# Value blocks mixed per batch from strided weights, in place of pairs of batches from a channel-major copy

## The chip, the cores and the metric

The kernel runs on one core of a Trainium2 chip. The metric is the device time in microseconds (us); several runs are taken and their median is given.

## What is computed

Four batches, eight heads, 768 tokens of 64 channels. The tokens of a head are cut into 8 blocks of 96. A small 8x8 matrix per head (`sort_net`) is made nearly doubly stochastic by five rounds of exp and of row and column normalisation, and then mixes the blocks of k and v; attention runs inside each block, and a gated feed-forward layer follows.

```python
for _ in range(5):
    P = np.exp(P - P.max(-1)); P = P / P.sum(-1); P = P / P.sum(-2)
k_sorted = np.einsum('bhij,bhjcd->bhicd', P, k_b)
v_sorted = np.einsum('bhij,bhjcd->bhicd', P, v_b)
attn = softmax(scale * q_b @ k_sorted.T)          # within a block of 96
x = (attn @ v_sorted)  as 3072 tokens x 512
out = (silu(x @ w_gate) * (x @ w_val)) @ w_out    # 512 -> 1536 -> 512
```

## The kernel before, in words

Natural tiles hold one row per (head, block), so 64 partitions for a batch, and 96 tokens x 64 channels (`C`, `D`) along each partition. `load_kq` (L78) puts k of a batch in partitions 0 to 63 and q in 64 to 127; `load_v` (L85) puts the two batches of a pair in the two halves. All these loads, which convert float32 to bfloat16, and the weights' (`load_w`, wo) are issued from GpSimd's queue in the order of the text: kq0, v of pair 0, w_gate and w_val in six pieces each, kq1, w_out, kq2, v of pair 1, kq3. `natp` has two buffers, `vnp` one.

The normalisation (L131 to L138) runs on ScalarE and VectorE at the start, and its result is spread by 16 small matmuls (L148) into `rmix` and `vmix`, zero-padded mixing matrices: `rmix[b]` for k and q (L154), `vmix[p]` for a pair's v (L159).

Mixing and transposing are one matmul: a natural slice is the weight, a mixing matrix moves.

- `emit_kq(b)` (L185): for each of the 96 token positions, the 64 channels are the weight columns (next to each other in memory), with two matmuls into the two halves of the partitions. Eight positions fill a PSUM tile `tkq`, and `drain` copies it into `kqt`. There are 12 drains a batch.
- `emit_v(pair)` (L206): for each channel, the tokens are the weight columns. `emit_vch` (L199) first copies the natural tile into `vch`, channel-major, so that they lie next to each other; a row of `vch` is padded from 96 to 128 with zeros (L119). VectorE makes the four copies of pair 0, GpSimd those of pair 1. Then 64 matmuls of 128 rows, 128 weight columns and 128 moving columns (two batches x 8 heads x 8 blocks) fill 16 PSUM tiles `tv` of four channels, each drained into `vt`, which has a 65th column of ones for the softmax sum.

`drain` (L178) takes VectorE and ScalarE in turn. The tiles `tkq`, `tv`, `qk`, `x_ps` and `w_ps` share three PSUM buffers (tag `att`).

`emit_qk` (L221) makes the scores of two heads for four blocks: weights of 64 rows, 128 columns (96 used, the other 32 are the next block's or a pad), and exp on ScalarE into `e_ring`, whose rows have a zeroed pad. `emit_av` (L240) multiplies by `vt`, divides by the sum, and transposes into `xt`. `emit_gv` (L282) is the gate and value layer, `emit_out` (L303) the output layer with its stores.

`emit_att(b)` (L261) emits the keys, then eight units of `emit_qk` and, two units behind, `emit_av`; after the second unit `emit_v` is emitted, in batches 0 and 2 alone. The last loop emits attention of batch b+1 ahead of the feed-forward of batch b. The order on each engine is set by a scheduler at build time, from the dependencies and its own estimates: it puts `g_ps` and `v_ps` matmuls of one batch between the attention steps of the next. On the chip each engine then works in that order.

Of the kernel before, what the change touches and what calls it, by code (L numbers as in the profile page):

```python
# [9 lines left out]
FP32 = mybir.dt.float32  # L10
# [7 lines left out]
def kernel(  # L18
# [36 lines left out]
    natp = ctx.enter_context(tc.tile_pool(name="natp", bufs=2))  # L55
    vnp = ctx.enter_context(tc.tile_pool(name="vnp", bufs=1))
# [28 lines left out]
    def load_v(pair, parts):  # L85
        t = vnp.tile([128, C, D], BF16, name=f"v{pair}", tag="vn")
        step = C // parts
        for s in range(parts):
            for u in range(2):
                nc.gpsimd.dma_start(out=t[u * R:(u + 1) * R, s * step:(s + 1) * step],  # L90
                                    in_=v_nat[2 * pair + u, :, s * step:(s + 1) * step])
        v_tiles[pair] = t
# [24 lines left out]
    vmix = [const.tile([128, 2, H, NB], BF16, name=f"vmix{p}") for p in range(B // 2)]  # L117
    vch = const.tile([128, D, 128], BF16, name="vch")
    nc.vector.memset(vch[:, :, C:], 0.0)  # L119
    for p in range(B // 2):  # L120
        nc.vector.memset(vmix[p], 0.0)
# [5 lines left out]
    load_v(0, 2)  # L127
# [23 lines left out]
    for b in range(B):  # L151
        wk = w_ps[0:R, :, b].unsqueeze(1).to_broadcast([R, H2, NB])
        for two in range(2):
            nc.vector.tensor_tensor(  # L154
                rmix[b][0:R, two, 0],
                mask[0:R].rearrange("p (g two) -> p two g", two=2)[:, two].unsqueeze(2).to_broadcast([R, H2, NB]),
                wk, op=ALU.mult)
        lo = (b % 2) * R
        nc.vector.tensor_tensor(  # L159
            vmix[b // 2][lo:lo + R, b % 2],  # L160
            mask[lo:lo + R].unsqueeze(2).to_broadcast([R, H, NB]),
            w_ps[lo:lo + R, :, b].unsqueeze(1).to_broadcast([R, H, NB]), op=ALU.mult)
# [7 lines left out]
    load_kq(1, [0, 48, 96])  # L170
    nc.gpsimd.dma_start(out=wo_sb, in_=wo_dram)
    load_kq(2, [0, 48, 96])
    load_v(1, 2)
    load_kq(3, [0, 48, 96])

    tog = [0]

    def drain(dst, src):  # L178
        if tog[0] % 2 == 0:
            nc.vector.tensor_copy(dst, src)  # L180
        else:
            nc.scalar.copy(dst, src)  # L182
        tog[0] += 1
# [15 lines left out]
    def emit_vch(pair):  # L199
        nat = v_tiles[pair]  # L200
        for s in range(4):
            cs = slice(s * (C // 4), (s + 1) * (C // 4))
            eng = nc.gpsimd if pair else nc.vector
            eng.tensor_copy(vch[:, :, cs], nat[:, cs, :].transpose([0, 2, 1]))  # L204

    def emit_v(pair):  # L206
        emit_vch(pair)
        dst = vtp.tile([C, 2 * H * NB, D + 1], BF16, name=f"vt{pair}", tag="vt")
        nc.vector.memset(dst[:, :, D:D + 1], 1.0)
        mix = vmix[pair].rearrange("p u a b -> p (u a b)")  # L210
        for db in range(D // 4):
            tp = psum.tile([128, 4, 2 * H * NB], FP32, name="tv", tag="att")
            for ld in range(4):
                nc.tensor.matmul(tp[:, ld, :], lhsT=vch[:, db * 4 + ld, :],  # L214
                                 rhs=mix, start=True, stop=True)
            drain(dst[:, :, ts(db, 4)], tp[0:C].transpose([0, 2, 1]))
        return dst.rearrange("p (u h i) d -> p u h i d", u=2, h=H)

    vts = {}
# [41 lines left out]
    def emit_att(b):  # L261
# [4 lines left out]
        for half, g in units:  # L266
# [3 lines left out]
            if vt is None and len(pend) == 2:  # L270
                if b % 2 == 0:
                    vts[b // 2] = emit_v(b // 2)
                vt = vts[b // 2][:, b % 2]
# [79 lines left out]
```

## Time and profile before

| what | value |
|---|---|
| median of three runs (lowest, highest) | 287.63 us (286.65, 287.9) |
| the profiled execution's own time | 287.63 us |
| its span, first to last instruction | 285.9 us |
| mean granted TensorE clock | 0.968 |
| matmul groups g_ps, v_ps, o_ps (L288, L297, L308) | 84.8, 82.1, 62.4 us busy |
| tkq, qk, av_ps, tv, x_ps (L193, L230, L245, L214, L255) | 20.3, 14.0, 14.9, 12.4, 11.5 us busy |
| drains of tv into vt: VectorE, ScalarE | 16 x 785 ns, 16 x 787 ns |
| drains of tkq into kqt: VectorE, ScalarE | 24 x 688 ns, 24 x 586 ns |
| GpSimd DMA loads | 14.16 MB written, slices 1 to 10 |

A group line names the source line, the engine, the operation, what it writes and reads, shapes, and the number; after the bar its busy time, the mean of one in ns, and the engine's idle time before it. PE is TensorE's matmul, PEld its weight load, DVE VectorE, ACT ScalarE, POOL GpSimd. A matmul's own duration contains the way through the array, and matmuls overlap; the spacing of a run of n is the run's time less one's duration, over n - 1. A timeline line has the start, the time of a run of like instructions, and in brackets the engine's idle time before it with what ended it. Slices are fortieths of the span; a line of a stretch has the stretch, then each engine's busy time and count, the granted clock, the DMA share and GB/s.

### The profile page before, as it was taken

What the parts mean: (1) busy time and instruction counts of PE and PEld (TensorE: products, weight loads), DVE (VectorE), ACT (ScalarE), POOL (GpSimd) and SP (SyncE); (2) the same over time, 40 slices, a digit from 0 to 9 for tenths busy, and PEclk for the clock granted to TensorE, in tenths of its full rate; (3) what the DMA queues carried; (4) which work ended last, traced back from release to release, by engine and by line L of the source; (5) the groups of instructions that cost most, each with busy time, mean ns of one, the idle gap of its engine ahead of it and who ended that gap; (6) DMA issues with size and microseconds to landing.
All of it is one profiled execution on the core that took longest, in us unless ns stands there. A gap on an engine that the chain in (4) does not pass through costs nothing.

```text
span 285.9 us, 6221 instructions
## 1 busy us (share of the span) xinstructions
PE 257.2 (90%) x2600; PEld 152.7 (53%) x2608; DVE 178.9 (63%) x383; ACT 121.7 (43%) x246; POOL 39.1 (14%) x51
## 2 busy tenths in 40 slices
PE   0077799969999999999999999999999999999993
PEld 0066555746655446666655446666555445555441
DVE  6798746937988205789988304699885018888300
ACT  2036745437633215976534215764332134343211
POOL 8557421029500000000000000000000000000000
PEclk9999955979999999999999999999999999999999
DMA  6999999999100122000000122000000220000021
GB/s 99 198 203 197 200 213 204 220 214 214 38 0 1 39 110 76 2 2 0 3 0 2 38 110 76 2 2 2 0 0 2 111 102 10 0 0 3 37 110 73
DMA packets 13659, 20.84 MB, mean 73 GB/s; under 512 B 1088, under 2 KB 8768, under 8 KB 13632
## 3 DMA queue, kind: packets, MB, share of 16 engines
q0 software_dynamic: 10128, 14.16, 28.2%
q1 hardware_dynamic: 3504, 6.30, 5.8%
q8 instruction: 20, 0.33, 0.4%
q14 instruction: 7, 0.06, 0.1%
HBM read 28.32 MB, written 6.29 MB: 121 GB/s over the span
## 4 chain that ended last, share of the span: by engine, by line
PE 82%; DVE 11%; ACT 3%; issue 2%; ACTq 0%
PE v_ps L297 22%; PE g_ps L288 22%; PE o_ps L308 22%; PE av_ps L245 4%; PE qk L230 4%; PE tkq L193 3%; PE x_ps L255 3%; PE tv L214 3%; DVE kqt L180 2%; DVE vch L204 1%; DVE st L251 1%; ACT vt L182 1%; DVE vt L180 1%; ACT th_sb L291 1%; DVE colred L136 0%
## 5 line engine op out<-in xcount | busy, mean ns | idle before, releaser
L288 PE MATMUL g_ps<-xt,wg_sb 128*128 128x384 bf16 x384 | 84.8, 331 | 0.2 <-DVE h L299 0.2
L297 PE MATMUL v_ps<-xt,wv_sb 128*128 128x384 bf16 x384 | 82.1, 331 | 0.0
L291 ACT ACTIVATE th_sb<-g_ps 128x384 bf16<-128x384 f32 x96 | 47.1, 491 | 63.2 <-PE g_ps L288 62.6
L293 DVE SCALAR_TENSOR_TENSOR gs_sb<-th_sb,g_ps 128x384 bf16<-128x384 bf16 x96 | 52.9, 551 | 26.9 <-ACT th_sb L291 20.9
L308 PE MATMUL o_ps<-wo_sb,h 128*128 128x512 bf16 x280 | 62.4, 379 | 0.4
L299 DVE SCALAR_TENSOR_TENSOR h<-v_ps,gs_sb 128x384 bf16<-128x384 f32 x96 | 53.1, 553 | 9.0 <-PE v_ps L297 0.8
L297 PEld LDWEIGHTS <-wv_sb 128*128 128x128 bf16 x384 | 36.8, 98 | 24.5 <-issue 0.8
L288 PEld LDWEIGHTS <-wg_sb 128*128 128x128 bf16 x384 | 36.2, 99 | 23.5 <-issue 2.3
L308 PEld LDWEIGHTS <-h 128*128 128x128 bf16 x288 | 28.2, 98 | 33.6
L180 DVE CAST kqt<-tkq 128x512 bf16<-128x512 f32 x24 | 15.9, 688 | 33.9 <-PE tkq L193 33.9
L311 ACT COPY o_sb<-o_ps 128x512 f32<-128x512 f32 x24 | 14.1, 586 | 51.4 <-PE o_ps L308 51.4
L235 ACT ACTIVATE er<-qk 96x384 bf16<-96x384 f32 x64 | 27.1, 487 | 12.2 <-PE qk L230 12.2
L193 PE MATMUL tkq<-rmix,kq 128*64 128x64 bf16 x768 | 20.3, 212 | 5.5 <-issue 2.5
L193 PEld LDWEIGHTS <-kq 128*64 128x64 bf16 x768 | 17.7, 126 | 8.9 <-issue 7.9
L251 DVE TENSOR_TENSOR st<-av_ps,r_sb 96x512 bf16<-96x512 f32 x32 | 21.9, 684 | 0.8
L182 ACT CAST kqt<-tkq 128x512 bf16<-128x512 f32 x24 | 14.1, 586 | 15.7 <-PE tkq L193 15.6
L230 PE MATMUL qk<-kqt 64*128 64x96 bf16 x256 | 14.0, 217 | 1.9 <-DVE kqt L180 1.4
L245 PE MATMUL av_ps<-vt,er 96*128 96x65 bf16 x256 | 14.9, 202 | 0.2 <-ACT vt L182 0.2
L180 DVE CAST vt<-tv 96x512 bf16<-96x512 f32 x16 | 12.2, 785 | 2.7 <-PE tv L214 2.5
L182 ACT CAST vt<-tv 96x512 bf16<-96x512 f32 x16 | 12.5, 787 | 2.1 <-PE tv L214 1.8
L214 PE MATMUL tv<-vmix,vch 128*128 128x128 bf16 x128 | 12.4, 236 | 1.0 <-DVE vt L180 0.3
L255 PEld LDWEIGHTS <-st 96*128 96x128 bf16 x128 | 7.6, 101 | 10.5 <-DVE st L251 9.1
(43 smaller groups left out, 123.0 us busy)
## 6 DMA issues: line engine op xcount, KB each, us to landing
out_dram<-o_sb SPq DMA_DIRECT2D x24, 256.0 KB, 2.0
v<-in_v_dram POOLq DMA_DIRECT2D x8, 384.0 KB, 13.1
kq<-in_k_dram POOLq DMA_DIRECT2D x6, 384.0 KB, 11.6
kq<-in_q_dram POOLq DMA_DIRECT2D x6, 384.0 KB, 12.1
wg_sb<-in_moe_w_gate_dram POOLq DMA_DIRECT2D x6, 256.0 KB, 11.8
wv_sb<-in_moe_w_val_dram POOLq DMA_DIRECT2D x6, 256.0 KB, 11.1
wo_sb<-in_moe_w_out_dram POOLq DMA_DIRECT2D x1, 1536.0 KB, 18.9
kq<-in_k_dram POOLq DMA_DIRECT2D x4, 192.0 KB, 5.6
```

Source lines behind the costliest of these rows:

```text
L180: nc.vector.tensor_copy(dst, src)
L182: nc.scalar.copy(dst, src)
L193: nc.tensor.matmul(tp[two * D:(two + 1) * D, lc, :], lhsT=nat[:, cb * 8 + lc, :], rhs=rm[:, two, :], start=True, stop=True)
L230: nc.tensor.matmul(pss[two][:, i4, :], lhsT=flat[lo:lo + D, at:at + 128], rhs=kqt[lo:lo + D, 1, g, i, :], start=True, stop=True)
L235: nc.scalar.activation(e[:, 0:4 * C], pss[two][0:C].rearrange("p a c -> p (a c)"), AF.Exp, scale=scale)
L245: nc.tensor.matmul(av[:, two, i4, :], lhsT=es[two][:, i4 * C:i4 * C + 128], rhs=vt[:, 2 * g + two, half * 4 + i4, :], start=True, stop=True)
L288: nc.tensor.matmul(g_ps, lhsT=wg_sb[:, kc, ts(m, 128)], rhs=xt[:, kc, :], start=(kc == 0), stop=(kc == NKC - 1))
L291: nc.scalar.activation(th_sb, g_ps, AF.Tanh, scale=0.5)
L293: nc.vector.scalar_tensor_tensor(gs_sb, th_sb, 1.0, g_ps, op0=ALU.add, op1=ALU.mult)
L297: nc.tensor.matmul(v_ps, lhsT=wv_sb[:, kc, ts(m, 128)], rhs=xt[:, kc, :], start=(kc == 0), stop=(kc == NKC - 1))
L299: nc.vector.scalar_tensor_tensor(h_w[:, m, :], v_ps, 0.5, gs_sb, op0=ALU.mult, op1=ALU.mult)
L308: nc.tensor.matmul(o_ps, lhsT=h_w[:, m, ts(t3, 128)], rhs=wo_sb[:, m, :], start=(m == 0), stop=(m == NFC - 1))
```

## The change

Value mixing goes batch by batch, straight from the natural tile. `vch`, its pad and its eight copies go. The natural v tile is 128 tokens long, the last 32 zeroed, and 128 tokens of one channel, 64 elements (128 bytes) apart, are the weight; only the 64 partitions of the batch take part, and `vmix` has no zero half and 64 moving columns. So a batch has 64 matmuls of 64 rows, 128 weight columns and 64 moving columns, eight to a PSUM tile, and 8 drains: 256 matmuls in place of 128, 32 drains as before. `emit_v` is emitted in each batch. v is loaded per batch, batch 0 in four parts of 16 partitions, the others in one of 64, batch 1 ahead of w_out; `natp` has three buffers, `vnp` two. Scores and attention-value products are as before.

```diff
-    natp = ctx.enter_context(tc.tile_pool(name="natp", bufs=2))
-    vnp = ctx.enter_context(tc.tile_pool(name="vnp", bufs=1))
+    natp = ctx.enter_context(tc.tile_pool(name="natp", bufs=3))
+    vnp = ctx.enter_context(tc.tile_pool(name="vnp", bufs=2))
...
-    def load_v(pair, parts):
-        t = vnp.tile([128, C, D], BF16, name=f"v{pair}", tag="vn")
-        step = C // parts
+    def load_v(b, parts):
+        if b % 2 == 0:
+            v_tiles[b] = vnp.tile([128, 128, D], BF16, name=f"v{b}", tag="vn")
+            nc.vector.memset(v_tiles[b][:, C:, :], 0.0)
+        else:
+            v_tiles[b] = v_tiles[b - 1]
+        lo = (b % 2) * R
+        n = R // parts
         for s in range(parts):
-            for u in range(2):
-                nc.gpsimd.dma_start(out=t[u * R:(u + 1) * R, s * step:(s + 1) * step],
-                                    in_=v_nat[2 * pair + u, :, s * step:(s + 1) * step])
-        v_tiles[pair] = t
+            nc.gpsimd.dma_start(out=v_tiles[b][lo + s * n:lo + (s + 1) * n, 0:C],
+                                in_=v_nat[b, s * n:(s + 1) * n])
...
-    vmix = [const.tile([128, 2, H, NB], BF16, name=f"vmix{p}") for p in range(B // 2)]
-    vch = const.tile([128, D, 128], BF16, name="vch")
-    nc.vector.memset(vch[:, :, C:], 0.0)
-    for p in range(B // 2):
-        nc.vector.memset(vmix[p], 0.0)
+    vmix = [const.tile([128, H, NB], BF16, name=f"vmix{b}") for b in range(B)]
...
-    load_v(0, 2)
+    load_v(0, 4)
...
     load_kq(1, [0, 48, 96])
+    load_v(1, 1)
     nc.gpsimd.dma_start(out=wo_sb, in_=wo_dram)
     load_kq(2, [0, 48, 96])
-    load_v(1, 2)
+    load_v(2, 1)
     load_kq(3, [0, 48, 96])
+    load_v(3, 1)
...
-    def emit_v(pair):
-        emit_vch(pair)
-        dst = vtp.tile([C, 2 * H * NB, D + 1], BF16, name=f"vt{pair}", tag="vt")
+    def emit_v(b):
+        nat = v_tiles[b]
+        lo = (b % 2) * R
+        dst = vtp.tile([C, H * NB, D + 1], BF16, name=f"vt{b}", tag="vt")
         nc.vector.memset(dst[:, :, D:D + 1], 1.0)
-        mix = vmix[pair].rearrange("p u a b -> p (u a b)")
-        for db in range(D // 4):
-            tp = psum.tile([128, 4, 2 * H * NB], FP32, name="tv", tag="att")
-            for ld in range(4):
-                nc.tensor.matmul(tp[:, ld, :], lhsT=vch[:, db * 4 + ld, :],
-                                 rhs=mix, start=True, stop=True)
-            drain(dst[:, :, ts(db, 4)], tp[0:C].transpose([0, 2, 1]))
-        return dst.rearrange("p (u h i) d -> p u h i d", u=2, h=H)
+        for db in range(D // 8):
+            tp = psum.tile([128, 8, H * NB], FP32, name="tv", tag="att")
+            for ld in range(8):
+                nc.tensor.matmul(tp[:, ld, :], lhsT=nat[lo:lo + R, :, db * 8 + ld],
+                                 rhs=vmix[b][lo:lo + R].rearrange("p a b -> p (a b)"),
+                                 start=True, stop=True)
+            drain(dst[:, :, ts(db, 8)], tp[0:C].transpose([0, 2, 1]))
+        return dst.rearrange("p (h i) d -> p h i d", h=H)
...
             if vt is None and len(pend) == 2:
-                if b % 2 == 0:
-                    vts[b // 2] = emit_v(b // 2)
-                vt = vts[b // 2][:, b % 2]
+                vt = emit_v(b)
```

## The prediction, as it was made

> **What bounds the kernel now.** I read the page first: shares, then the slices, then the chain that ended last.
>
> ```profile
> span 285.9 us, 6221 instructions
> PE 257.2 (90%) x2600; PEld 152.7 (53%) x2608; DVE 178.9 (63%) x383; ACT 121.7 (43%) x246; POOL 39.1 (14%) x51
> PE   0077799969999999999999999999999999999993
> PEclk9999955979999999999999999999999999999999
> PE v_ps L297 22%; PE g_ps L288 22%; PE o_ps L308 22%; PE av_ps L245 4%; PE qk L230 4%; PE tkq L193 3%; PE x_ps L255 3%; PE tv L214 3%; DVE kqt L180 2%; DVE vch L204 1%; DVE st L251 1%; ACT vt L182 1%; DVE vt L180 1%; ACT th_sb L291 1%; DVE colred L136 0%
> ```
>
> One slice is 7.15 us. From slice 7 on TensorE is full: there any nanosecond added to it is added to the end, and work taken off other engines is worth nothing. The first five slices differ: the chain runs over kqt, vch and vt, so DVE and ACT decide there. The change touches both regions with opposite signs, and I price them apart. The profiled execution took 287.63 us, which is also the median of the three times shown; 1.7 us lie outside the span.
>
> The timeline of the first region shows what the v copies hold up:
>
> ```profile
> 1.25 0.91 DVE L119 MEMSET vch<- 128x1024 uint32 x1 [0.17 <-issue]
> ...
> 15.93 0.69 DVE L180 CAST kqt<-tkq 128x512 bf16<-128x512 f32 x1
> ...
> 16.65 1.51 DVE L204 COPY vch<-v 128x1536 bf16<-128x1536 bf16 x1
> ...
> 23.88 1.47 DVE L204 COPY vch<-v 128x1536 bf16<-128x1536 bf16 x1
> 24.08 0.61 PEld L230 LDWEIGHTS <-kqt 64*128 64x128 bf16 x13 [1.55 <-ACT kqt L182]
> ...
> 25.57 4.18 PE L214 MATMUL tv<-vmix,vch 128*128 128x128 bf16 x36
> ```
>
> **Part 1, start of the scale chain: +0.75 us.** DVE clears pads before it can reduce p_sb. Before: vch 0.91 and two vmix (0.18 together), 1.09 us. After: two v pads of the same 1024 words each, about 0.91 apiece, 1.82 us, ahead of the first reduction at 2.56. ScalarE's exp ends at 2.53, so there is no slack. The difference is 0.73, say 0.75; every later step of the five iterations moves with it.
>
> **Part 2, copies leave DVE: -2.5 us.** Four copies of about 1.49 us stand between the kqt drains in DVE's queue. Without them I laid the twelve drains out again by rows: 0.69 on DVE, 0.59 on ScalarE in turn, 0.43 us of tkq matmuls for each (53 ns a pair in this stretch) and three PSUM buffers. DVE can start at 15.93; the last drain ends near 21.7, and the first score weights load near 21.9 instead of 24.08: -2.2. If TensorE is quicker, DVE's own six drains still take to 20.1, and the gain is at most 3.8. I take -2.5. The four copies on POOL go too and are worth nothing: their output is not read before 116 us, 40 us after they end.
>
> **Part 3, the first value stage is halved.** Now batch 0 waits for the mix of two batches: 16 drains, from 25.57 to the end of the last at 33.62, 8.05 us. After the change it is 8 drains, each for 8 matmuls. A drain then has the form of kqt's (runs of 8 along d), and may fall from 0.79 to 0.69 and 0.59. How long the stage lasts depends on c, the spacing of the new matmuls.
>
> **The unknown: c.** The new weights are one d of 128 tokens, 128 bytes apart. No weight load in this trace is strided. The rows nearest to it from the two sides:
>
> ```profile
> 66.35 0.34 PE L255 MATMUL x_ps<-ident,st 96*128 96x96 bf16 x4
> 66.62 0.20 PEld L230 LDWEIGHTS <-kqt 64*128 64x128 bf16 x8
> 66.62 0.34 PE L230 MATMUL qk<-kqt 64*128 64x96 bf16 x8
> ...
> 66.90 0.43 PE L245 MATMUL av_ps<-vt,er 96*128 96x65 bf16 x8
> ```
> ```profile
> L204 POOL COPY vch<-v 128x1536 bf16<-128x1536 bf16 x4 | 11.2, 2878 | 0.0
> ...
> L204 DVE COPY vch<-v 128x1536 bf16<-128x1536 bf16 x4 | 6.0, 1490 | 0.0
> ```
>
> Low end: eight av matmuls, 128 contiguous weight columns, 65 moving columns, 0.43 us less one's 0.193 over seven steps: 33 ns. High end: the same v read at the same stride by DVE, 1490/1536 = 0.97 ns an element; a load that reads 128 columns one by one at that rate takes 124 ns. (POOL's is 1.87, 240 ns a load; I give it little weight, as POOL is the slower in the same copy.) The av row is nearest in operation, the copy in access pattern; I find no reason to prefer one and take their geometric mean, c = 64 ns, an estimate.
>
> Two pages of the Trainium skill pull apart here. "TensorE: Matmul & The Clock Gate", Weight-path perf modes, says that the fast load applies to 128 columns of a 16-bit type, packed or strided, which speaks for the low end; that the 96 used columns are padded to 128 would then keep it on. "SBUF — State Buffer", Door 1 (cachelines), speaks against the change: full bandwidth needs two hits on a 16-byte line, and here each column is on a line of its own. By a halved fast load of 32 steps at 1.2 GHz an estimate from the two is 53 ns; the sum below would end 2.8 us lower.
>
> **Part 3 priced.** A group of 8 takes 0.51 us at c = 64, longer than the 0.39 that two draining engines need for one. So the stage is 8 x 0.51 + 0.9 (latency and last drain) = 5.0 against 8.05: -3.05. At c = 33, with TensorE still at its slow spacing here (N=64 about 53 ns, as tkq shows), 4.6: -3.4. At 124: 8.8, +0.8.
>
> **Part 4, TensorE where it is full.** Batches 1, 2, 3 each get 64 matmuls, 192 in all; the 64 of pair 1 go, at 55 ns each (four, 0.39 us less 0.219, over three). So +192c - 3.5. At 64: 12.3 - 3.5 = +8.8. Each batch's 8 drains lie beside gv matmuls.
>
> **Part 5, changes of array shape: +2.3 us.** The lines at 66 us show a second cost. x_ps starts at 66.35, and its four need 0.17 (0.34 - 0.206 + 0.043); scores, which have 64 rows, start 0.27 later: 0.10 lost. Out of the scores as much is lost: the last of the eight starts 0.14 after the first (0.34 - 0.20), and av another 0.14 later, where the spacing is 0.04. Between tv and v_ps nothing is: 116.36 to 116.59 is four times 56. The new tv has 64 rows, so it is no longer free to alternate with the g and v matmuls. In the changed instruction order batches 1 to 3 have 12 blocks of tv between g and v matmuls: 24 changes at 0.095 = +2.3.
>
> **Part 6, a stall that goes: -1.5 us.** Pair 1's stage runs from 116.36 to 124.08, 7.72 us, for 64 x 0.055 + 16 x 0.162 of g and v = 6.1: 1.5 of it waits for drains. At c = 64 TensorE is slower than the drains; the wait goes (at 33 about half stays).
>
> **Transfers: nothing.** v of batch 1 moves behind kq1 and the weights come earlier; v of batch 0 comes in four parts of 16 partitions. The present v, twice the bytes, lands by 20.4; the new need is at 23.8 (24.08 - 2.5 + 0.75, and 1.49 of scores as now). If the narrow parts ran at half rate they would still land by then; if not, each us late is a us on the start. The third kq buffer lets kq3 (behind POOL's 9.8 us wait at 62) be issued early; TensorE doesn't wait for kq3 now. vt becomes four tiles in two buffers: batch 2's first write waits for the last av of batch 0, over 50 us earlier.
>
> **Sum at c = 64:** 0.75 - 2.5 - 3.05 + 8.8 + 2.3 - 1.5 = +4.8, so 287.6 + 4.8 = **292.4 us**.
>
> Open on both sides: the granted clock.
>
> ```profile
> 33.60:54.00 20.40, 19.07 (x180) 11.01 (x179) 12.61 (x29) 8.97 (x22) 4.34 (x9) 0.67 1.17 212
> ```
>
> In this stretch (clock 0.67 in the third column from the end) the clock is half for 13.7 us, and the units of attention run every 2.5 us; I estimate 0.8 us less each for some five units if the spell goes, -4, and the same up if it doubles. A pause of 2.54 us in tkq at 57.4, released by nothing that the profile shows, may also go or come again. I set both at 0.
>
> **Rivals.**
> - Loads nearly as quick as contiguous ones (c under 45, priced at 33), the case on the other side: 0.75 - 2.5 - 3.4 + (6.3 - 3.5) + 2.3 - 0.7 = -0.75, 286.9. With the larger gain of part 2 it is 285.6, and this mechanism decides once c is under about 37 ns, where the sum is zero. For it: the load is the same instruction with as many columns. Against it: every strided read of v in the trace runs near or above 1 ns an element. Chance 0.25.
> - The padding does not buy a fast load, and columns come one by one (c over 90, priced at 124): 0.75 - 2.5 + 0.8 + (23.8 - 3.5) + 2.3 - 1.5 = +20.2, 307.8. Then the change doesn't do what its name says, for v. For it: DVE's row. Against it: contiguous loads run at a quarter of that a column. Chance 0.25; POOL's rate or worse, over 330 us, 0.05.
> - My forecast, c between 45 and 90, by the same sum 288.9 to 299: chance 0.45.
>
> **Range.** 285.0 (the quick load and a little from clock or pause) to 307.8. What a measurement of this kernel can tell from no change is about 0.5%, 1.4 us. Of the 0.25 of the first rival about 0.13 lies under 286.2, 0.10 within, the rest above; of the middle 0.02 lies within. Faster 0.13, same 0.12, slower 0.75.
>
> **What would show it.** The tv group: spacing in one run of 8 (c itself), 256 matmuls; score weights loaded near 22.3 us (parts 1 and 2); first av near 29 (part 3); about 95 ns lost at each end of a tv block; vt drains at 0.59 to 0.69. Wrong if tv's spacing is at 33 or over 100 ns, if v lands after 23.8 us, or if the half clock lasts otherwise.

## The result, and the profile after

The change makes the kernel slower: 305.47 us (median of four runs, 304.23 to 305.73) against 287.39 (four runs, 286.65 to 287.90), ratio 1.0623 with a 95% interval of 1.0585 to 1.0661. The profiled execution took 304.23 us with a span of 302.4; before, 287.63 and 285.9. So 16.5 us of span have to be found, where the prediction had 4.8.

The page of the changed kernel, for the lines shown of before (a slice is now 7.56 us):

```profile
span 302.4 us, 6473 instructions
PE 277.7 (92%) x2728; PEld 168.8 (56%) x2736; DVE 173.3 (57%) x380; ACT 122.2 (40%) x246; POOL 24.8 (8%) x46
PE   0188899899999999999999999999999999999994
PEclk9995559957999999669999999669999999999998
PE v_ps L288 22%; PE g_ps L279 22%; PE o_ps L299 20%; PE tv L208 8%; PE tkq L194 4%; PE av_ps L238 4%; PE qk L223 4%; PE x_ps L248 3%; DVE st L244 1%; DVE kqt L181 1%; ACT kqt L183 1%; DVE v L88 1%; ACT th_sb L282 0%; DVE colred L135 0%; ACT er L228 0%
L208 PE MATMUL tv<-vmix,v 64*128 64x64 bf16 x256 | 25.4, 266 | 0.0
L181 DVE CAST vt<-tv 96x512 bf16<-96x512 f32 x16 | 11.3, 708 | 18.4 <-PE tv L208 18.4
L183 ACT CAST vt<-tv 96x512 bf16<-96x512 f32 x16 | 11.3, 705 | 15.6 <-PE tv L208 15.6
```

In the chain tv has grown from 3% to 8%, and vch and vt have left it. The drains of tv wait 18.4 and 15.6 us for TensorE: the producer is now the slow side. The clock row is new in kind: besides the half-clock spell of the start there are three more dips, in slices 9 and 10, 17 and 18, and 26 and 27. In each value stage of batches 1, 2 and 3 (they start at 58.19, 119.80 and 188.92 us) the granted clock falls to one half 2.4 to 3.4 us after the start and stays there for 10.24 us, past the stage's end: from 61.62, 123.06 and 191.32 us. Such a stretch of half clock is called a spell below. Before had only one, of 3.41 us at 59.53, besides the first (13.65 us from 35.64; after, 20.48 from 24.07) and the last few us, which both kernels have.

The start, from the timeline of the changed kernel:

```profile
2.62 0.91 DVE L88 MEMSET v<- 128x1024 uint32 x1 [0.16 <-issue]
3.45 0.15 DVE L132 TENSOR_REDUCE rowred<-p_sb 32x8 f32<-32x64 f32 x1
...
21.55 0.37 PEld L223 LDWEIGHTS <-kqt 64*128 64x128 bf16 x13 [0.79 <-ACT kqt L183]
...
23.68 0.30 PE L223 MATMUL qk<-kqt 64*128 64x96 bf16 x3 [1.00 <-issue]
23.91 5.89 PE L208 MATMUL tv<-vmix,v 64*128 64x64 bf16 x64
...
30.56 0.60 PE L238 MATMUL av_ps<-vt,er 96*128 96x65 bf16 x8 [0.17 <-ACT vt L183]
```

The unknown c can be read at 23.91: 64 matmuls in 5.89 us, one of them 0.27 long, give (5.89 - 0.27)/63 = 89 ns. The clock is half there; a stage on both sides of a clock change shows whether that matters, in batch 3:

```profile
188.65 0.34 PE L288 MATMUL v_ps<-xt,wv_sb 128*128 128x384 bf16 x1
188.92 0.91 PE L208 MATMUL tv<-vmix,v 64*128 64x64 bf16 x8
189.76 0.34 PE L288 MATMUL v_ps<-xt,wv_sb 128*128 128x384 bf16 x1
190.03 1.64 PE L208 MATMUL tv<-vmix,v 64*128 64x64 bf16 x16
191.60 0.50 PE L279 MATMUL g_ps<-xt,wg_sb 128*128 128x384 bf16 x1
192.04 1.61 PE L208 MATMUL tv<-vmix,v 64*128 64x64 bf16 x16
```

Up to 191.3 a g or v matmul lasts 0.34, after it 0.50: the clock has halved. The tv blocks of 16 take 1.64 and 1.61 us on the two sides, (1.64 - 0.27)/15 = 91 ns and as much. So the spacing of the new matmuls doesn't follow TensorE's clock, and it is 90 ns.

The page hides where the time went; stretches between the starts of the blocks of o_ps, one block per batch, show it. The first stretch holds the start and the value stages of batches 0 and 1, the second that of batch 2, the third that of batch 3; the fourth has none.

| us | to o0 | o0 to o1 | o1 to o2 | o2 to o3 |
|---|---|---|---|---|
| before | 94.04 | 64.54 | 59.49 | 47.55 |
| after | 97.41 | 69.12 | 68.63 | 47.55 |

The fourth is equal to 0.01 us. The third is the cleanest, since before had no value stage there: +9.14 us for 64 matmuls. In the rows of stretches (busy time and count by engine, granted clock in the third column from the end) it is before

```profile
158.58:218.07 59.49, 58.78 (x612) 34.20 (x612) 37.60 (x74) 26.50 (x56) 0.00 (x0) 1.00 0.08 28
```

and after, with the spell itself as a second row

```profile
166.53:235.16 68.63, 67.92 (x673) 40.79 (x674) 40.23 (x78) 29.84 (x61) 0.00 (x0) 0.93 0.07 24
191.32:201.56 10.24, 10.24 (x74) 6.59 (x74) 4.02 (x7) 4.26 (x8) 0.00 (x0) 0.50 0.00 1
```

By the forecast's terms 64 x 0.090 + 8 x 0.095 = 6.5 of the 9.14 are loads and changes of shape. The other 2.6 belong with a clock of 0.93.

### The profile page after: what moved, and what is told of

It is laid out like the page before. It is cut to its first block, busy times and chain, and to the rows that moved or that the text cites. A ratio compares the mean times of both kernels' runs of the same rounds, so it can differ in the third digit from the quotient of the medians.

```text
span 302.4 us, 6473 instructions
## 1 busy us (share of the span) xinstructions
PE 277.7 (92%) x2728; PEld 168.8 (56%) x2736; DVE 173.3 (57%) x380; ACT 122.2 (40%) x246; POOL 24.8 (8%) x46
## 2 busy tenths in 40 slices
DMA packets 13388, 20.86 MB, mean 69 GB/s; under 512 B 1072, under 2 KB 8752, under 8 KB 13104
## 3 DMA queue, kind: packets, MB, share of 16 engines
q0 software_dynamic: 9856, 14.16, 27.9%
## 4 chain that ended last, share of the span: by engine, by line
PE 88%; DVE 7%; ACT 3%; issue 2%; ACTq 0%
PE v_ps L288 22%; PE g_ps L279 22%; PE o_ps L299 20%; PE tv L208 8%; PE tkq L194 4%; PE av_ps L238 4%; PE qk L223 4%; PE x_ps L248 3%; DVE st L244 1%; DVE kqt L181 1%; ACT kqt L183 1%; DVE v L88 1%; ACT th_sb L282 0%; DVE colred L135 0%; ACT er L228 0%
## 5 line engine op out<-in xcount | busy, mean ns | idle before, releaser
L279 PE MATMUL g_ps<-xt,wg_sb 128*128 128x384 bf16 x384 | 87.3, 341 | 0.2 <-DVE h L290 0.2
L288 PE MATMUL v_ps<-xt,wv_sb 128*128 128x384 bf16 x384 | 86.8, 340 | 0.0
L288 PEld LDWEIGHTS <-wv_sb 128*128 128x128 bf16 x384 | 37.7, 100 | 25.7 <-issue 2.0
L228 ACT ACTIVATE er<-qk 96x384 bf16<-96x384 f32 x64 | 27.7, 485 | 15.7 <-PE qk L223 15.6
L208 PEld LDWEIGHTS <-v 64*128 64x128 bf16 x256 | 23.8, 209 | 3.6 <-issue 3.6
L208 PE MATMUL tv<-vmix,v 64*128 64x64 bf16 x256 | 25.4, 266 | 0.0
L181 DVE CAST vt<-tv 96x512 bf16<-96x512 f32 x16 | 11.3, 708 | 18.4 <-PE tv L208 18.4
L194 PE MATMUL tkq<-rmix,kq 128*64 128x64 bf16 x768 | 18.8, 208 | 2.6 <-DVE kqt L181 0.9
L194 PEld LDWEIGHTS <-kq 128*64 128x64 bf16 x768 | 16.8, 122 | 5.3 <-issue 4.3
L183 ACT CAST kqt<-tkq 128x512 bf16<-128x512 f32 x24 | 14.0, 586 | 11.6 <-PE tkq L194 11.5
L183 ACT CAST vt<-tv 96x512 bf16<-96x512 f32 x16 | 11.3, 705 | 15.6 <-PE tv L208 15.6
L223 PE MATMUL qk<-kqt 64*128 64x96 bf16 x256 | 15.0, 224 | 2.2 <-issue 1.0
## 6 DMA issues: line engine op xcount, KB each, us to landing
kq<-in_q_dram POOLq DMA_DIRECT2D x6, 384.0 KB, 19.1
```

What stands on the lines that cost most here:

```text
L194: nc.tensor.matmul(tp[two * D:(two + 1) * D, lc, :], lhsT=nat[:, cb * 8 + lc, :], rhs=rm[:, two, :], start=True, stop=True)
L208: nc.tensor.matmul(tp[:, ld, :], lhsT=nat[lo:lo + R, :, db * 8 + ld], rhs=vmix[b][lo:lo + R].rearrange("p a b -> p (a b)"), start=True, st ...
L228: nc.scalar.activation(e[:, 0:4 * C], pss[two][0:C].rearrange("p a c -> p (a c)"), AF.Exp, scale=scale)
L279: nc.tensor.matmul(g_ps, lhsT=wg_sb[:, kc, ts(m, 128)], rhs=xt[:, kc, :], start=(kc == 0), stop=(kc == NKC - 1))
L288: nc.tensor.matmul(v_ps, lhsT=wv_sb[:, kc, ts(m, 128)], rhs=xt[:, kc, :], start=(kc == 0), stop=(kc == NKC - 1))
```

## The experiments

Theory: a load of 128 columns that lie 128 bytes apart takes 90 ns whatever the array does, and that alone is the larger part; a value stage that is slow and fills only half of the array's rows also brings the half clock. Rivals: the split into batches (64 rows, changes of shape, more and smaller matmuls) costs the time and not the stride; 64 rows make the load slow; the half clock is an accident of one run. The last is weak from the outset: the four executions of the changed kernel were granted 0.912 to 0.918 of the clock in the mean, before 0.968. The theories are weighed by spacing of the tv matmuls, stretches between o_ps blocks, and spells. Kernel "before" ran beside them at 286.0, 286.1, 286.1 and 285.9 us in the four groups.

### Batches split, but loads contiguous

The changed kernel keeps its batches, 64 rows and 64 moving columns, and takes its weights from a channel-major copy again.

```diff
+    vch = const.tile([128, D, 128], BF16, name="vch")
+    nc.vector.memset(vch[:, :, C:], 0.0)
...
+        eng = nc.gpsimd if b >= 2 else nc.vector
+        h0 = (b % 2) * R
+        for s in range(4):
+            cs = slice(s * 24, (s + 1) * 24)
+            eng.tensor_copy(vch[h0:h0 + R, :, cs], nat[h0:h0 + R, cs, :].transpose([0, 2, 1]))
...
-                nc.tensor.matmul(tp[:, ld, :], lhsT=nat[lo:lo + R, :, db * 8 + ld],
+                nc.tensor.matmul(tp[:, ld, :], lhsT=vch[lo:lo + R, db * 8 + ld, :],
```

> The changed kernel, but its 64-row value matmuls read contiguous weights: the channel-major copy is back (VectorE for batches 0 and 1, GpSimd for 2 and 3; two kq buffers). Theory A (the stride makes each load 90 ns, and the slow loads let the clock drop to half after each value stage): spacing of tv 30 to 35 ns at full clock, the three half-clock spells of 10.2 us behind the value stages of batches 1 to 3 are gone; 305.5 - 192 x 0.057 (10.9) - 8 (clock) + 2.5 (copies) - 1.5 (first stage) = about 287.5 us. Rival B (64 rows, not the stride, make the load slow): spacing stays at 90, 303 or more. Rival C (array-shape changes and the new order cost the time): spacing 33, yet 298 or more.

Measured: 288.43 us, ratio 1.0106 (1.0061 to 1.0152). No spell comes with the stages of batches 2 and 3. In batch 3, with the row of its stretch between o_ps blocks below:

```profile
179.95 0.64 PE L214 MATMUL tv<-vmix,vch 64*128 64x64 bf16 x16
180.52 0.34 PE L285 MATMUL g_ps<-xt,wg_sb 128*128 128x384 bf16 x1
180.79 0.72 PE L214 MATMUL tv<-vmix,vch 64*128 64x64 bf16 x16
...
182.03 0.87 PE L214 MATMUL tv<-vmix,vch 64*128 64x64 bf16 x24
```
```profile
156.95:219.17 62.22, 61.55 (x677) 36.13 (x675) 39.86 (x78) 29.36 (x61) 0.00 (x0) 1.00 0.07 27
```

24 matmuls in 0.87, one of them some 0.2 long, are 29 ns apart. The third stretch took 62.22 us, 2.73 over before: 64 x 0.029 + 8 x 0.095 = 2.62. That is parts 4 and 5 of the prediction with another c, and next to nothing is left over. The split by itself costs about 1%; the strided loads and what comes with them cost the other 5%.

### Strided loads, but batches in pairs

Before, with its 128 rows and 128 moving columns, reads the natural tile (padded to 128 tokens) and makes no copy.

```diff
-        emit_vch(pair)
+        nat = v_tiles[pair]
...
-                nc.tensor.matmul(tp[:, ld, :], lhsT=vch[:, db * 4 + ld, :],
+                nc.tensor.matmul(tp[:, ld, :], lhsT=nat[:, :, db * 4 + ld],
```

> The kernel before, pair by pair with 128 rows and 128 moving columns, but the weights come strided from the natural tile (padded to 128 tokens), with no copies. Theory A: spacing 90 in place of 55; pair 0's stage stays bound by its drains and the copies' 2.5 us go; pair 1's stage gains 64 x 35 ns = 2.2 less 1.5 of waits, and up to 3 if a half-clock spell follows it: 285 to 289 us. Rival B: spacing 55 as before, 284 us. Rival C: no loss at all, since no array-shape change is added, 284 us.

Measured: 284.32 us, ratio 0.9942 (0.9915 to 0.9970), 0.6% under before. The theory had 285 to 289 and its rivals 284, so the time alone doesn't speak for the theory; the rows do. The first stretch is 90.24, 3.80 less than before (no copies on VectorE; 2.5 was expected); the second is 65.87, 1.33 more (128 columns move, as before, and spacings of 55 and of 88 to 94 ns stand side by side within a PSUM tile). No spell comes with pair 1's stage. Strided loads are thus not a loss by themselves: it depends on how many there are, and on what else the matmul fills.

### A ruler for the step

The changed kernel, with the distance of the weight columns changed from stage to stage; these loads read other places of v, so the mixed values are others and only the spacing is read. Batch 2 loads 96 columns, batch 3 has 128 rows.

```diff
+        steps = [64, 32, 16, 8, 4, 2, 1, 64] if b else [64] * 8
+        cols = C if b == 2 else 128
+        rows = slice(0, 128) if b == 3 else slice(lo, lo + R)
...
+                w = flat[rows, 0:128 * s].rearrange("p (c s) -> p c s", s=s)[:, 0:cols, (db * 8 + ld) % s]
```

> A ruler, not a candidate: in batches 1 to 3 the eight groups of eight value matmuls read weights 64, 32, 16, 8, 4, 2, 1 and 64 elements apart (from wrong places of the v tile, so the mixed v is wrong); batch 1 with 64 rows and 128 columns, batch 2 with 64 rows and the 96 columns that are used, batch 3 with 128 rows and 128 columns. Theory A: spacing near 33 at step 1, the same with 64 and with 128 rows, and 90 at step 64; if 16-byte lines are the cause, it is flat from step 8 up and falls below that. Rival B: 90 at every step with 64 rows, near 33 with 128 rows. With 96 columns: three quarters of 90 (68 ns) if the load goes column by column, more than 90 if 128 columns buy a faster load for strided weights too.

The timeline of batch 3 has blocks of 8 at step 64, 16 at steps 32 and 16, 16 at 8 and 4, and 24 at 2, 1 and 64; batch 2's first block, at step 64 with 96 columns, stands ahead of them:

```profile
119.77 1.49 PE L215 MATMUL tv<-vmix,v 64*96 64x64 bf16 x8
...
192.09 0.85 PE L215 MATMUL tv<-vmix,v 128*128 128x64 bf16 x8
...
192.94 1.14 PE L215 MATMUL tv<-vmix,v 128*128 128x64 bf16 x16
...
194.08 0.88 PE L215 MATMUL tv<-vmix,v 128*128 128x64 bf16 x16
...
195.46 1.35 PE L215 MATMUL tv<-vmix,v 128*128 128x64 bf16 x24
```

Seven steps of the first 128-row block share 0.85 less the 0.2 of one, which is 93 ns; the blocks fall with the step. Start to start the matmuls are, with those of the second ruler and at full clock where nothing else is said:

| columns apart, elements of 2 bytes | 1, 2, 3 | 4 | 5 | 6 | 7 | 8 to 63 | 64 |
|---|---|---|---|---|---|---|---|
| ns, 128 columns | 29 | 31 | 40 | 46 | 53 | 58 to 66 (24: 70) | 91 to 95 |
| ns, 96 columns | 80 (1 and 2, half clock) | 90 (half clock) | | | | 163 (32), 180 (16), 177 (8, half clock) | 163 |

64 rows and 128 rows give the same (95 and 93 at step 64, 61 and 66 at 32). So the rival by which 64 rows make the load slow falls. Padding to 128 columns pays: 96 columns at step 64 cost 163 ns, 128 cost 92. But a padded strided load is still at least three times a contiguous one; the 29 ns are no more than the matmul of 64 moving columns takes by itself (53 at half clock), so the contiguous load may be shorter still.

Two pages of the Trainium skill, cited in the prediction, meet their numbers here. "TensorE: Matmul & The Clock Gate", Weight-path perf modes, says that loads of 128 columns of a 16-bit type, packed or strided, take the fast way; 92 against 163 ns agrees, though "strided" is not the speed of "packed". "SBUF — State Buffer", Door 1, wants two hits on each line of 16 bytes; up to step 4 (two columns on a line) the load hides behind the matmul, at step 8 (one) it takes 62. That agrees; the same box's other figure, 8 bf16 as the stride that costs nothing, does not. The second rise, at 128 bytes, is on neither page, and with 96 columns there is none.

```diff
+        steps = [[64] * 8, [64, 63, 60, 56, 48, 40, 36, 33],
+                 [64, 63, 60, 56, 48, 40, 36, 33], [28, 24, 20, 12, 7, 6, 5, 3]][b]
```

> A second ruler (weights from wrong places of the v tile, so the mixed v is wrong): batch 1 (64 rows) and batch 2 (128 rows) read weights 64, 63, 60, 56, 48, 40, 36 and 33 elements apart, batch 3 (128 rows) 28, 24, 20, 12, 7, 6, 5 and 3. The first ruler gave 62 to 65 ns from step 8 to 32, about 92 at 64, 29 to 31 up to step 4. If a 16-byte line for each column is all, every step from 8 up is at 62 and 64 alone stands out (a power of two, one bank). If the distance counts, the spacing grows from 33 to 64. Steps 5 to 7 lie between 31 and 62 if it is lines touched.

This second ruler (again values from other places; batches 2 and 3 on 128 rows) shows that the second rise isn't gradual: 63 elements cost 58 ns on 64 rows and 64 on 128, 64 elements cost 91 to 95. No spell comes with its batches 2 and 3, both on 128 rows.

### The same loads on 128 rows

Batches 1 to 3 of the changed kernel use all 128 rows; the mixing matrix is zero in the other batch's half, so the result is unchanged.

```diff
+    for b in range(1, B):
+        nc.vector.memset(vmix[b], 0.0)
...
+        rows = slice(0, 128) if b else slice(0, R)
...
-                nc.tensor.matmul(tp[:, ld, :], lhsT=nat[lo:lo + R, :, db * 8 + ld],
-                                 rhs=vmix[b][lo:lo + R].rearrange("p a b -> p (a b)"),
+                nc.tensor.matmul(tp[:, ld, :], lhsT=nat[rows, :, db * 8 + ld],
+                                 rhs=vmix[b][rows].rearrange("p a b -> p (a b)"),
```

> The changed kernel, but in batches 1 to 3 the value matmuls use all 128 rows (the mixing matrix is zero for the other batch's half), so that tv no longer changes the array's shape. Theory A: spacing stays at 90 and the half-clock spells stay; 24 shape changes at 0.095 us go: 305.5 - 2.3 = 303.2 us. Rival B: spacing falls to 33 to 55 and the time to about 290. Rival C: the time falls by much more than 2.3 us with the spacing as it is.

Measured: 292.04 us, ratio 1.0216 (1.0162 to 1.0270). I had put it near 303; the spells of the stages are gone, and that I had not expected.

```profile
181.82 0.83 PE L211 MATMUL tv<-vmix,v 128*128 128x64 bf16 x8
182.48 0.33 PE L291 MATMUL v_ps<-xt,wv_sb 128*128 128x384 bf16 x1
182.65 1.53 PE L211 MATMUL tv<-vmix,v 128*128 128x64 bf16 x16
```

The spacing stays, (1.53 - 0.24)/15 = 86 to 92 ns over the blocks, and between tv and v_ps nothing is lost. The third stretch runs at full clock:

```profile
159.52:224.35 64.83, 64.23 (x677) 39.77 (x675) 40.18 (x78) 29.75 (x61) 0.00 (x0) 1.00 0.07 26
```

It is 5.34 over before, a little less than 64 x 0.090 = 5.8, and 3.80 under after. Of these 3.80, 0.76 are changes of shape, and 3.04 the half clock. This is the cleanest separation of the terms: same loads, same number, same order, only the rows differ. Over the whole span it saves 302.4 - 291.6 = 10.8 us; 2.3 of that are changes of shape, and about 8.5 the clock. (The two profiled executions are the shortest of the changed kernel and the longest of this one; by the two ratios the difference is 11.6 us, so 8.5 is rather too little.)

### What of the half-filled array brings the half clock?

One further idea was that the amount of multiplying decides, so that 128 moving columns would do what 128 rows did. Here the 64-row matmuls move the mix twice; the second result isn't read.

```diff
-    vmix = [const.tile([128, H, NB], BF16, name=f"vmix{b}") for b in range(B)]
+    vmix = [const.tile([128, 2, H, NB], BF16, name=f"vmix{b}") for b in range(B)]
...
+        nc.scalar.copy(vmix[b][lo:lo + R, 1], vmix[b][lo:lo + R, 0])
...
-        for db in range(D // 8):
-            tp = psum.tile([128, 8, H * NB], FP32, name="tv", tag="att")
+        for db in range(D // 4):
+            tp = psum.tile([128, 4, 2 * H * NB], FP32, name="tv", tag="att")
```

> The changed kernel with 64 rows and strided weights as they are, but each value matmul moves 128 columns: the mixing matrix stands there twice, and the second half of the result is not read (four channels to a PSUM tile, 16 half-size drains a batch). Theory A, as it stands after the first four runs (the load of 90 ns sets the spacing; the clock drops because too few cells of the array work, rows x columns, in the value stages): spacing stays at 90 though the moving columns double, the half-clock spells behind the value stages of batches 2 and 3 go: 305.5 - 2 x 3.2 - 1.5 + 1.1 (12 more shape changes) = about 298.7 us. Rival D (the number of rows alone, or something else in the 64-row form, brings the spells): spells stay, 306 or more. Rival E (load and matmul are in series): spacing rises by 27 to 117, 310 or more.

Measured: 308.12 us, ratio 1.0807 (1.0725 to 1.0889). Spacing is 85 to 97 ns at full clock, and spells of 13.65 and 10.24 us still come with the stages of batches 2 and 3. In batch 3 the g matmuls show it, 0.34 us and then 0.50:

```profile
193.87 0.34 PE L280 MATMUL g_ps<-xt,wg_sb 128*128 128x384 bf16 x1
194.14 1.95 PE L209 MATMUL tv<-vmix,v 64*128 64x128 bf16 x16
196.02 0.50 PE L280 MATMUL g_ps<-xt,wg_sb 128*128 128x384 bf16 x1
```

So 128 moving columns on 64 rows don't do what 64 columns on 128 rows did, and what I expected of the idea fell. The idea itself isn't ruled out by it: the stages are also longer here, 9.4 and 9.2 us against 6.5, with six blocks of tv and their changes of shape; the 128-row stages had four blocks and no such changes. The sum at the end of this section takes it up again.

The next puts batch 2 alone on 96 rows.

```diff
+        rows = slice(0, 96) if b == 2 else slice(lo, lo + R)
```

> The changed kernel with 96 rows in place of 64 for the value matmuls of batch 2 alone (the mixing matrix is zero for the 32 more). Rival D in two forms. The array's 64-row form (which also costs 0.095 us at each change) brings the spell: with 96 rows neither the changes' cost nor the spell at about 123 us is there, the spell of batch 3 at about 187 is. If it is the number of rows at work, a spell of the same or half the length stays. Spacing 90 in both.

Measured in a single execution: 302.56 us. With 96 rows there is no loss at a change of shape, spacing is still 90, and the spell of batch 2 is 6.83 us (from 125.45, where the stage of 119.46 to 125.98 ends) in place of 10.24; batch 3, left at 64 rows, keeps its 10.24. Between 64 and 128 rows the spell is thus of a length between. The stretch ahead of it, and the spell:

```profile
122.04:125.45 3.41, 3.41 (x39) 3.28 (x38) 1.98 (x4) 1.93 (x3) 0.00 (x0) 1.00 0.02 5
125.45:132.28 6.83, 6.83 (x47) 3.67 (x46) 2.73 (x6) 2.13 (x4) 0.00 (x0) 0.50 0.00 0
```

The last has 64 rows and 128 moving columns, as above, but contiguous weights from a copy.

```diff
+            eng.tensor_copy(vch[h0:h0 + R, :, cs], nat[h0:h0 + R, cs, :].transpose([0, 2, 1]))
...
-                nc.tensor.matmul(tp[:, ld, :], lhsT=nat[lo:lo + R, :, db * 8 + ld],
+                nc.tensor.matmul(tp[:, ld, :], lhsT=vch[lo:lo + R, db * 4 + ld, :],
```

> What brings the half-clock spells: 64 rows alone, or 64 rows that stand idle between slow loads. The kernel with contiguous 64-row weights, with 128 moving columns (the mixing matrix twice, the second half of the result not read): the rows are kept moving, at 55 ns a matmul, and the stages are about as long as 16 half drains take, 5 us or more with the g and v matmuls between. If slow loads (idle between) are needed for a spell, none of 10 us behind the stages of batches 2 and 3, and about 293 us. If half the rows are enough when the stage is long, spells as with strided weights, 298 us or more.

Measured in a single execution: 300.17 us. By the time alone this would be a case of 298 us or more, the one with spells; about 293 was expected without. But a stage takes 6.1 us at a spacing of 55 ns, and no spell comes with batches 2 and 3. The row of batch 3's stretch is at full clock:

```profile
166.00:230.68 64.68, 63.86 (x677) 37.71 (x674) 40.93 (x82) 30.56 (x65) 0.00 (x0) 1.00 0.07 26
```

The time lies elsewhere: against the first experiment, which has the same copies, the first stretch is 6.6 us longer (101.17 against 94.59), of which the stages of batches 0 and 1, with their 128 moving columns and 16 drains, are 3.3 and 2.4, and the other two stretches with a stage are 2.5 each.

(Between 53 and 64 us most kernels, before included, have a spell in or after the keys of batch 1, whatever their value stages; so the comparison is of batches 2 and 3.) Neither 64 rows alone nor slow loads alone bring the spell of these stages; both together do.

One sum orders these runs, and all the traces with them. Within a trace, every change of the clock lies a whole number of times 3.41 us from every other. So I cut each of the fourteen traces into such stretches and added up what the array multiplied in each: 0.42 ns for every moving column (a g or v matmul of 384 columns takes 162 ns at full clock), weighted by its rows and its weight columns as shares of 128. A stretch with the whole array at work at full clock has 100%. In the stretch ahead of the spell of batch 3 the changed kernel has 27%, ahead of those of batches 1 and 2 it has 21 and 22%. The stages of batch 2 in the other runs:

| run | sum in the stretches of 3.41 us | clock behind them |
|---|---|---|
| 64 rows, 128 columns, strided | 34% | half |
| 96 rows, strided | 37%, then 34% | full, then half |
| 128 rows, strided | 40%, 41% | full |
| 64 rows, 128 columns, contiguous | 42%, 50% | full |
| 64 rows, 64 columns, contiguous | 56%, 51% | full |

Over all traces, from 40 us to 12 us before the end, there are 962 such stretches. Behind 66 of them the clock is half, and their sums go up to 37.8%; behind 896 it is full, and theirs start at 36.6%; seven lie where the two overlap. Without the weights the groups don't part: by moving columns alone 128 strided rows (41%, full) would have to fall before 64 rows with 128 columns (52%, half). So in these traces the clock follows what the array multiplied in the 3.41 us before, and few rows, few moving columns and slow loads all lower it. This is a reading of the traces, made after the runs; no run was made to test it.

### Two row groups in turn, and a pitch that avoids 128 bytes

The pair's two batches alternate matmul by matmul between rows 0 to 63 and 64 to 127, in case the two loads overlap.

```diff
+                for ld in range(8):
+                    for u in range(2):
+                        rows = slice(u * R, (u + 1) * R)
+                        nc.tensor.matmul(tps[u][:, ld, :], lhsT=nat[rows, :, db * 8 + ld],
+                                         rhs=vmix[b + u][rows].rearrange("p a b -> p (a b)"),
```

> The changed kernel's 64-row matmuls, but a pair's two batches take turns, one in rows 0 to 63 and one in 64 to 127, in the stages of batches 0 and 2 (as scores do it). Theory A (the load's way out of SBUF is the limit, 92 ns for 128 columns 128 bytes apart, for each row half by itself): two loads overlap and the mean spacing falls to about 46 ns; if the two halves' loads follow each other it stays at 92. Rival D (one idle half of the rows brings the half-clock spell): no spell behind pair 1's stage, since both halves work. With 46 ns and no spell about 289 us, first stage longer by 3 (two batches at the start); with 92 ns and a spell 303.

Measured: 299.08 us, ratio 1.0418 (1.0345 to 1.0491). In the one profile, which is of the longest of the four executions, a pair of matmuls takes 2 x 73 ns on average against 2 x 90: the loads overlap in part. A spell of 17.07 us is there from 122.28, against what rival D expected; the other three executions were granted 0.925 to 0.942 of the clock in the mean, before beside them 0.973 to 0.985. By the sum above the stretch ahead of this spell has 27%: both halves work, but 64 rows at a time.

The next lays v out with 66 elements from token to token, which the rulers price at 61 ns.

```diff
-            v_tiles[b] = vnp.tile([128, 128, D], BF16, name=f"v{b}", tag="vn")
+            t = vnp.tile([128, 128, D + 2], BF16, name=f"v{b}", tag="vn")
...
+            v_tiles[b] = t[:, :, 0:D]
```

> The changed kernel with one size changed: a token takes 66 elements (132 bytes) in the v tile in place of 64. The ruler gave 58 to 65 ns for steps from 8 to 63 and 92 at 64. If 64 is special as a power of two, spacing is near 61: 192 x 0.03 = 5.8 us and 1.5 in the first stage less, 298 us, with the spells where they are; 291 if the shorter stages bring no spells. If all steps from 64 up cost 92, no change, 305.

Measured: 303.66 us, ratio 1.0615 (1.0584 to 1.0645), the same as the changed kernel. The spacing is 61 ns as expected, and a stage of batch 2 or 3 takes 6.0 us in place of 7.6, but the gain is given back. On its page:

```profile
DMA packets 37708, 20.86 MB, mean 69 GB/s; under 512 B 25648, under 2 KB 33328, under 8 KB 37680
...
q0 software_dynamic: 34176, 14.16, 61.9%
```

The packets are 37,708 where the changed kernel has 13,388, and GpSimd's queue takes 61.9% of the engines' span in place of 27.9%: the 24,320 more are the 24,576 tokens less their 256 rows, so a pitch of 132 bytes breaks every token out of its row. v of batch 0 lands at 25.57 us in place of 19.13. The first tv starts at 27.55, not 23.91, and the pause ahead of the last three scores, 1.00 us in the changed kernel, is 4.82:

```profile
27.32 0.42 PE L224 MATMUL qk<-kqt 64*128 64x96 bf16 x3 [4.82 <-issue]
27.55 4.12 PE L209 MATMUL tv<-vmix,v 64*128 64x64 bf16 x64
```

The trace's packets show what such pauses go with. Queue 8, which the page calls "instruction", moves a packet of 16 KB now and then; here one runs from 24.26 to 25.95 us, and TensorE goes on at 27.32. In the changed kernel one ends at 22.07 (TensorE goes on at 23.68), in before one at 58.44, ahead of the end of its pause in tkq (59.90). In all traces there are 20 pauses of TensorE of more than 0.45 us (0.48 to 4.82) that are put to "issue", and each ends 1.3 to 1.7 us after such a packet. So TensorE seems to wait for its next instructions, which come late among v's packets; no run tried it.

The start is thus 2.4 us longer (99.80 us to o0 against 97.41). In the third stretch only 0.85 of 64 x 0.029 = 1.86 us comes out (67.78 against 68.63): the spell is as long as it was and covers more of the work that slows in it, since fewer of the loads fall into it (32 of 64, against 41). The same pitch in the faster paired kernel:

```diff
-        t = vnp.tile([128, C, D], BF16, name=f"v{pair}", tag="vn")
+        t = vnp.tile([128, 128, D + 2], BF16, name=f"v{pair}", tag="vn")
+        nc.vector.memset(t[:, C:, :], 0.0)
+        t = t[:, :, 0:D]
```

> A candidate: the pair kernel with strided 128-row weights and no copies (0.994 of before), with a token pitch of 66 elements. Spacing in pair 1's stage falls from 92 to 61 where loads set it, 64 x 0.03 = 1.9 us, of which some returns as waits for drains (1.5 in the kernel before): 0.4 to 1.9 us under the pair kernel, ratio to before 0.987 to 0.993. No change if 66 costs as 64 does.

Measured: 288.00 us, ratio 1.0052 (1.0022 to 1.0082), a miss: I had expected 0.987 to 0.993. v lands at 26.18 in place of 20.55, and TensorE waits for it (tv starts at 26.31, not 22.65). A layout that TensorE likes can be one that the transfer doesn't.

### Strided weights for pair 0, a copy for pair 1

Strided loads where VectorE bounds (pair 0), GpSimd's copy where TensorE does (pair 1); o_sb has two buffers in place of three to make room.

```diff
-        emit_vch(pair)
+        nat = v_tiles[pair]
+        if pair:
+            emit_vch(pair)
...
+                nc.tensor.matmul(tp[:, ld, :], lhsT=vch[:, db * 4 + ld, :] if pair else nat[:, :, db * 4 + ld],
```

> A candidate: the kernel before with strided weights for pair 0 alone (its stage waits for drains anyway), and GpSimd's channel-major copy for pair 1, whose stage lies where TensorE is full; two output buffers in place of three for room. Theory A: as the pair kernel with strided weights, less what its second stage was longer than before (8.56 against 7.57 us): 1.0 us under that run, ratio to before about 0.991, 283.5 us where before is 286. If the strided loads cost nothing in the second stage either, no difference to that run.

Measured: 283.85 us, ratio 0.9951 (0.9911 to 0.9992): 0.5% under before, and not to be told from the paired strided kernel (0.9942), where 0.991 was expected. Its first stretch, 88.64 us, is 5.4 less than before's. The second, 65.03, is half a microsecond above before's 64.54, so the 1.33 of the strided pair 1 is mostly saved. But the profiled execution is the shortest of the ten (282.6 us, a span of 280.8); I can't settle whether this version is the better of the two.

## Why the prediction was wrong

The sign was right, and 304 or 305 us lies inside 285.0 to 307.8; the size was wrong, 4.8 us forecast and 16.5 in the span. The rival of columns one by one ends nearer, at 307.8, but by chance: it had 124 ns a load, 34 more than there were, and no half clock. Term by term:

| term | forecast | measured |
|---|---|---|
| parts 1 and 2, score weights | -1.75 (22.3 us) | -2.5 (21.55 us) |
| pause ahead of the last three scores | 0 | +0.9 |
| part 3, first value stage | -3.05 (5.0 us) | -1.45 (6.6 us) |
| parts 4 and 6, 192c - 3.5, and the stall that goes | +8.8 - 1.5 | +13.8 - 1.5 by c = 90 |
| part 5, changes of shape | +2.3 | +2.3 |
| keys of batch 1 (tkq), where a pause of 2.54 us shrank to 0.62 | 0 | -2.3 |
| granted clock | 0 | about +8.5 |

With -0.5 after the last o_ps start, they sum to +17.2, 0.7 above the span's difference; the last tv of a block overlaps a little with what follows. The loads' and shapes' lines are counts times measured spacings, and the clock's is the difference to the run with 128 rows.

**Parts 1 and 2: part 2 right, part 1 too large.** The first reduction moved from 2.56 to 3.45 us, but lmix only from 12.85 to 13.05, 0.2 in place of 0.75: not every later step moved with it, since the first iteration, up to the second exp, took 2.20 us before and 1.58 after (why isn't shown). The gain of the copies was about 2.7, and 2.5 was forecast.

**Part 3: the mechanism was right, the size was the failed c.** The first av starts at 30.56 in place of 33.67; forecast near 29. The line of before:

```profile
33.67 0.41 PE L245 MATMUL av_ps<-vt,er 96*128 96x65 bf16 x8 [0.20 <-ACT vt L182]
```

The stage takes 6.6 us, which is 8 x 0.71 + 0.9, the same formula with c = 90. The drains fell to 705 and 708 ns from 785 and 787, as expected in direction; 0.59 to 0.69 was forecast.

**Part 4, the first step that failed: "I find no reason to prefer one and take their geometric mean, c = 64 ns".** Measured 90, which was the upper edge of the case it was put in. The two rows were both of other things: a contiguous load and a VectorE copy. By the rulers, 64 is about the price of any step from 8 to 63 elements; 64 elements lie one past that. No row of before showed it, and the text should have let more of the weight stand at the upper end. It costs 5.0 us in part 4 and 1.6 in part 3.

**Part 5: right.** In the contiguous split 2.62 of 2.73 us are explained by it and by 64 spacings. At full clock, from a g or v matmul to tv the starts are 268 ns apart in place of 162.

**Part 6: right.** With c above the drains' pace, tv's drains wait for TensorE (18.4 and 15.6 us in their groups) and TensorE doesn't wait for them.

**The granted clock, the second and larger failure: "I set both at 0".** The clock was named as open and given 4 us to each side, for the spell that was visible, in the attention of batch 0. That spell did lengthen, from 13.65 to 20.48 us, and no run separates its price. But that new stages might bring spells of their own wasn't thought of. Three of 10.24 us came, and cost about 8.5 us by the 128-row experiment. A spell costs far less than half its length, 3.04 of 10.24 us in batch 3: g and v matmuls last 0.50 in place of 0.34 in it, but the strided loads run at 90 ns at either clock.

"The Trainium skill" has on its page "TensorE: Matmul & The Clock Gate", What's actually happening, that the gate opens with activity and closes after an idle window of about 3.4 us. The three spells are three times 3.41 us long, which agrees with the window. But no idle one stands ahead of them: in the stretch from 187.90 to 191.32 us TensorE shows matmuls for 3.34 of 3.42 us, and the next stretch is at half. So busy time as the records have it doesn't settle the clock. What the array multiplied in that stretch is 27% of what it could, and by the sum above that does; whether the gate counts just this stays open.

## What to carry to other kernels

Price a strided weight load by its step before the copy that it replaces is thrown away: here at most 29 ns up to 4 elements, about 60 from 8 on, 92 at 128 bytes, and nothing of it shrinks with fewer rows. Splitting a full-height matmul into half-height ones doubles the loads; where TensorE is full, that is paid in the end-to-end time, and here also in the clock. Before adding such a stage, add up what the array multiplies in 3.41 us of it: below about 37% of its full rate the clock was halved here. Use the strided form where another engine is late (the first phase) and keep the copy, on an idle engine, where TensorE is.

## What the runs showed of the hardware that was not expected

- Loads whose columns are 63 elements apart take 58 to 64 ns, 64 apart 91 to 95, on 64 rows and on 128; at half clock the second is about the same, 90.
- Loads of 96 contiguous columns are 80 ns apart (at half clock), more than the 62 of 128 strided ones.
- TensorE with hardly a gap can be granted half its clock, for spells of 10.24 us with strided 64-row stages, 6.83 with 96 rows, none with 128, and none with 64 rows and contiguous weights. In 955 of 962 stretches of 3.41 us the clock of the next goes with the share that the array multiplied: half below 36.6%, full above 37.8%.
- Pauses of TensorE of 0.48 to 4.82 us, 20 in the traces, each end 1.3 to 1.7 us after a 16 KB packet on the queue that the page calls "instruction".
- Loads into the two halves of the rows overlap only in part: 73 ns in turn, against 92.
- A destination pitch of 132 bytes in place of 128 raised the packets from 13,388 to 37,708 and put v's landing from 19.1 to 25.6 us.
